# Attention and feed-forward on one core: v of the last batch planned later, mask products a bank wide, the last output in column halves, priorities anew

## The chip, the core and the metric

The kernel runs on one core of one Trainium2 chip. A core has five engines with a queue of instructions each: TensorE (matmuls; PE in the profile, with its weight loads as PEld), VectorE (DVE), ScalarE (ACT), GpSimd (POOL) and SyncE (SP), and 16 DMA engines. POOL and SP issue the DMAs here. Matmuls write to PSUM, which has 8 banks of 2 KB a partition (512 fp32 columns); SBUF holds everything else. The metric is the time of one execution on the device in microseconds, lower is better.

## The reference

Two things follow one another: an attention with two fixed masks, and a feed-forward layer over its output.

```python
B, H, S, D = 8, 8, 576, 64
scores = q @ k.T / sqrt(D)                    # for each batch and head
rel = pos[:, None] - pos[None, :]
mask_local   = (rel >= 0) & (rel < 32)                        # heads 0 to 3
mask_strided = (rel >= 0) & (pos[None, :] % 32 == pos[:, None] % 32)  # heads 4 to 7
attn = softmax(where(mask, scores, -1e9))
x = (attn @ v), reshaped to 4608 tokens x 512
h = x @ w_in                                  # 512 -> 2048
g = s * max(h, 0)**2 + b
out = g @ w_out                               # 2048 -> 512, fp32
```

Inputs and output are fp32 in DRAM; the kernel computes in fp16 with sums in fp32.

## The kernel before

**How the work is cut.** A batch has two pairs of local heads (m = 0, 1) and two of strided heads (m = 2, 3). A local pair is 6 tiles of 96 queries; a tile sees its own 96 keys and the 32 before them, so 128 key rows. A strided pair is 8 tiles of 72: positions that are equal modulo 32 meet only each other, and four such classes share a tile of 72. Two heads lie side by side, so one scores product has 2 x 96 or 2 x 72 columns, and a PSUM bank takes two local tiles (384 columns) or three strided ones (432). `pair_steps` (L474) lists the TensorE steps of a pair: transposes of q and k (L494, L502, with the results copied or spread over tiles by `copy_on`, L404), scores (L623), the exponential on ScalarE (L641), the products with v (L684; a column of ones in v gives the sum of each row), reciprocal (L701) and normalising (L707 on ScalarE, six instructions of 96x64 a group, allowed for batch 0 only, or L711 on VectorE, one instruction), and the transposes of x (L731). In later batches the transposes of q, k and x are DMA transposes on SP's queue; q then goes through a spreading copy.

**The mask.** For batches 1 to 7 VectorE multiplies the exponentials by a mask of 0 and 1 (L649). For batch 0 (`b < PE_MASK`) TensorE writes the mask ahead of each scores product: identity times a row of 0 and -30000 (L620), with the scores product then added in the same columns of PSUM.

**v.** `fetch_v` (L1339) issues the loads of v of a batch on POOL's queue, four DMAs for local heads (L382) and, from batch 4 on, four for strided heads (L387). In the local form each tile of v has the last 32 rows of the tile before it as its first rows; `rows_before` (L435) copies them, in two instructions a batch, on ScalarE or VectorE (kind "in"). They are due when the plan expects the loads to have landed: `landing(4600)`.

**The feed-forward.** `ff1` (L973) multiplies 128 of 2048 rows by a block of 512 tokens (matmul L983, relu L1009 or L1011, square L1017 or L1019). The last two blocks (T = 7, 8) go through `ff1_seven` (L1087, matmul L1208), which forms the block product with seven half-size products in place of eight. `ff2` (L1229, matmul L1238) and, for later blocks, `ff2_seven` (L853, matmul L951; seven products P1 to P7) do the second product. In `ff2_seven` `ev` (L870) evicts sums that are used twice, `add_db` (L893) adds the bias part, and `store` (L878) evicts a quarter of the output block and issues its DMA on SP (L886). For the last block the bank W is in halves of 128 tokens, and its last product, P3, stores a half after each t.

**Order.** All of it is laid out at build time by a list scheduler, `Plan` (L19). It keeps a clock that TensorE's steps advance, times at which ScalarE, VectorE, GpSimd and the queues are planned to be free, and for each piece of work what it needs and what it costs. `flush` (L45) issues, out of the work that is ready, the piece with the smallest sum of its ready time and an offset in ns for its kind, `ORDER` (L124); work of batch 0 or of first tiles has no offset. An engine may be booked up to `SLACK` ahead. What TensorE does next is chosen in the main loop (L1508): a step of attention if it is ready and either attention is behind its due time (`due`, L1515) or nothing else is ready, else a step of `ff1` or `ff2`; in the head, small products of no use (L1502) keep TensorE running. PSUM banks are given out by `group_of` (L453): one bank for transposes (t), two for scores (s), one for sums over v (a), two each for `ff1` and `ff2`; for batch 0, scores may also use the `f1` banks. No search runs at build (`ORDERS = 0`), so the numbers in `ORDER` settle the order of all instructions.

Of the kernel before, what the change touches and what calls it, by code (L numbers as in the profile page):

```python
# [13 lines left out]
FP32 = mybir.dt.float32  # L14
# [4 lines left out]
class Plan:  # L19
# [98 lines left out]
class Step:  # L118
    def __init__(self, fn, ns, needs=(), group=None, keys=(), posts=(), after=None):
# [4 lines left out]
ORDER = {"g": 1500.0, "S": 2500.0, "in": 2500.0, "w_mix": 0.0, "wc": 1000.0, "ev": 1000.0,  # L124
# [3 lines left out]
         "u": 0.0, "SLACK": 600.0, "ahead": 0.05}  # L128
KINDS = ("g", "S", "in", "w_mix", "wc", "Va", "Ua", "Ub", "Vb", "C22", "xc", "q", "k", "r", "x", "e",
         "p", "u", "ev", "fv", "fu", "fe", "c11", "c22", "c21", "c12")  # L130


def varied(order, rnd):

    order = dict(order)
    for kind in rnd.sample(KINDS, rnd.choice((1, 2, 4))):
        order[kind] = rnd.choice((-1500.0, -800.0, -400.0, 0.0, 500.0, 1000.0, 1500.0, 2500.0))
    if rnd.random() < 0.2:
        order["SLACK"] = rnd.choice((400.0, 600.0, 800.0, 1000.0))
    if rnd.random() < 0.2:  # L140
        order["ahead"] = rnd.choice((0.0, 0.05, 0.1, 0.2))
    return order
# [46 lines left out]
def lay_out(ctx, tc, nc, q, k, v, moe_w_in, moe_w_out, moe_s, moe_b, out, order, q_shape, out_shape,  # L189
# [284 lines left out]
    def pair_steps(b, m):  # L474
# [135 lines left out]
        def score(i, group):  # L610
# [3 lines left out]
            def f():  # L614
                if i % per_s == 0:
                    st["s", g] = bank(group)
                c = i % per_s * 2 * nq
                if b < PE_MASK:

                    nc.tensor.matmul(  # L620
                        out=st["s", g][0:nk, c:c + 2 * nq], lhsT=ident[0:nk, 0:nk],
                        rhs=neg_loc if loc else neg_str, start=True, stop=False)
                nc.tensor.matmul(  # L623
                    out=st["s", g][0:nk, c:c + 2 * nq], lhsT=(st["k"][:, i * nq:i * nq + nk] if loc else st["k"][:, i, 0:SQ]),
                    rhs=st["q"][:, i].rearrange("d e c -> d (e c)"), start=b >= PE_MASK, stop=True)
# [227 lines left out]
    def ff2_seven(T):  # L853
# [24 lines left out]
        def store(i, k, of, plus, ts=slice(0, 2)):  # L878
            def g(eng):
                o = op.tile([128, 2, 256], FP32, tag="o", name="o")  # L880
                src = gts[of, T][:, ts] if (of, T) in gts else gts[of, T, ts.start]
                nc.vector.scalar_tensor_tensor(
                    out=o[:, ts], in0=src, scalar=s_sb[:, 0:1],
                    in1=plus()[:, ts], op0=ALU.mult, op1=ALU.add)
# [3 lines left out]
                        "(t p) m -> p t m", p=128)[:, ts], in_=o[:, ts])  # L888
# [707 lines left out]
```

## Time and profile before

| | |
|---|---|
| median of 3 runs | 298.67 us (298.17 to 298.99) |
| profiled execution | 298.86 us |
| its span, first to last instruction | 297.1 us |
| granted TensorE clock | 0.999 of full speed |
| TensorE busy from 9 to 20.4 us | 10.39 us |
| TensorE busy from 20.4 to 174 us | 153.60 of 153.6 us |
| TensorE busy from 174 to 204 us | 29.23 of 30 us |
| TensorE busy from 242 to 293.6 us | 51.58 of 51.6 us |
| last matmul ends | 293.58 us |
| last DMA, 128 KB of output, issued and landed | 294.13 and 296.18 us |

The first rows are the whole run; the stretches show where TensorE has gaps. The ends of matmuls are modelled, so "busy" is not "at its peak": how densely matmuls stand is read from their starts. A few lines of the costliest groups, with busy time and mean ns of one, then the idle time of the engine ahead of them and what ended it:

```profile
L983 PE MATMUL ps_f<-xT,w_in_sb 128*128 128x512 f16 (+4 forms) x568 | 115.5, 331 | 0.3 <-ACT u L1009 0.3
L1009 ACT ACTIVATE u<-ps_f 128x512 f16<-128x512 f32 x104 | 61.0, 594 | 32.5 <-PE ps_f L983 31.8
L951 PE MATMUL ps_f<-w_out_sb,gT 128*128 128x256 f16 x376 | 55.6, 273 | 0.0
L641 ACT ACTIVATE p_loc<-ps_s 128x384 f16<-128x384 f32 x46 | 21.4, 494 | 4.8 <-PE ps_s L623 4.3
```

TensorE's first product hardly ever waits (0.3 us in the whole run), and ScalarE's relu spends its idle time waiting for TensorE.

### The profile page before, as it was taken

The numbers are of one execution on the slowest core, as the hardware profiler recorded it, in microseconds if no ns is written. First come the engines' busy times: TensorE is split into PE (matmuls) and PEld (weight loads), VectorE is DVE, ScalarE is ACT, GpSimd is POOL, SyncE is SP. The second block draws the span as 40 slices with busy tenths as digits, with TensorE's granted clock in tenths as the row PEclk, the third lists the DMA queues.
The fourth block names the chain that finished last, engine by engine and source line by source line (L and its number), as shares of the span: only waits on it lengthen the run. The fifth ranks groups of instructions, "written<-read, shape, count | busy, mean of one in ns | idle before, by whom it ended". The sixth has DMA issues, their size and how long they took to land.

```text
span 297.1 us, 7092 instructions
## 1 busy us (share of the span) xinstructions
PE 290.5 (98%) x2802; PEld 220.0 (74%) x2802; DVE 235.3 (79%) x501; ACT 194.3 (65%) x336; POOL 93.7 (32%) x140
## 2 busy tenths in 40 slices
PE   8999999999999999999999999999999999999995
PEld 3775656666556568889767776768888989999984
DVE  5857888798966988787877896759898588888963
ACT  3577957898838798647774878469877545675400
POOL 8873624601980296009710394100000000000000
PEclk9999999999999999999999999999999999999999
DMA  8999999997999499989999999999230300110214
GB/s 136 189 206 203 218 180 184 223 171 119 109 195 149 67 132 138 170 173 122 148 136 144 182 170 105 143 140 207 44 97 0 108 29 9 71 38 3 95 48 142
DMA packets 106152, 38.19 MB, mean 129 GB/s; under 512 B 85414, under 2 KB 103974, under 8 KB 106118
## 3 DMA queue, kind: packets, MB, share of 16 engines
q0 software_dynamic: 60848, 18.23, 62.7%
q1 hardware_dynamic: 45270, 19.51, 36.0%
q8 instruction: 22, 0.36, 0.5%
q14 instruction: 12, 0.10, 0.1%
HBM read 36.99 MB, written 10.62 MB: 160 GB/s over the span
## 4 chain that ended last, share of the span: by engine, by line
PE 88%; DMA 6%; ACT 2%; DVE 2%; POOL 1%; issue 1%; ACTq 0%
PE ps_f L983 28%; PE ps_f L951 22%; PE ps_f L1238 8%; DMA v_loc<-in_v_dram 6%; PE ps_s L623 5%; PE ps_f L1208 3%; PE ps_a L684 3%; PE ps_s L1502 2%; PE ps_a L1208 2%; PE ps_s L951 2%; PE ps_t L1208 2%; PE ps_s L1208 2%; PE ps_t L951 1%; PE ps_s L1238 1%; PE ps_t L684 1%; PE ps_t L502 1%
## 5 line engine op out<-in xcount | busy, mean ns | idle before, releaser
L983 PE MATMUL ps_f<-xT,w_in_sb 128*128 128x512 f16 (+4 forms) x568 | 115.5, 331 | 0.3 <-ACT u L1009 0.3
L1009 ACT ACTIVATE u<-ps_f 128x512 f16<-128x512 f32 x104 | 61.0, 594 | 32.5 <-PE ps_f L983 31.8
L983 PEld LDWEIGHTS <-w_in_sb 128*128 128x128 f16 x576 | 57.4, 114 | 23.2 <-issue 0.5
L951 PEld LDWEIGHTS <-gT 128*128 128x128 f16 x608 | 58.4, 98 | 9.2
L951 PE MATMUL ps_f<-w_out_sb,gT 128*128 128x256 f16 x376 | 55.6, 273 | 0.0
L1017 ACT ACTIVATE gT<-u 128x1024 f16<-128x1024 f16 x29 | 30.7, 1057 | 0.8
L1238 PE MATMUL ps_f<-w_out_sb,gT 128*128 128x512 f16 x112 | 30.4, 379 | 0.0
L951 PE MATMUL ps_f<-w_mix,gT 128*128 128x256 f16 x176 | 25.1, 273 | 0.0
L641 ACT ACTIVATE p_str<-ps_s 72x432 f16<-72x432 f32 (+1 forms) x46 | 20.7, 482 | 6.4 <-PE ps_s L623 5.8
L711 DVE TENSOR_TENSOR x_nat<-ps_a,rec 96x384 f16<-96x384 f32 (+2 forms) x46 | 24.1, 523 | 0.6
L641 ACT ACTIVATE p_loc<-ps_s 128x384 f16<-128x384 f32 x46 | 21.4, 494 | 4.8 <-PE ps_s L623 4.3
L1019 DVE TENSOR_TENSOR gT<-u 128x1024 f16<-128x1024 f16 x27 | 18.5, 686 | 5.9 <-ACT u L1009 5.4
L819 DVE TENSOR_TENSOR gT<-gT 128x1024 f16<-128x1024 f16 x34 | 22.4, 678 | 0.6 <-ACT gT L1017 0.4
L382 POOL DMA_DIRECT2D v_loc<-in_v_dram x24 | 17.7, 757 | 8.6 <-DMA w_out_sb<-in_moe_w_out_dram 5.7
L951 PEld LDWEIGHTS <-S 128*128 128x128 f16 x176 | 17.1, 98 | 2.9
L1238 PEld LDWEIGHTS <-gT 128*128 128x128 f16 x128 | 11.4, 98 | 7.8
L387 POOL DMA_DIRECT2D v_str<-in_v_dram x16 | 13.0, 816 | 12.3 <-PE ps_f L983 3.6
L684 PEld LDWEIGHTS <-p_str 72*128 72x128 f16 x256 | 12.8, 98 | 5.1 <-ACT p_str L641 0.4
L1323 POOL COPY gate<-kT 1x1 f16<-1x1 f16 x6 | 1.5, 256 | 45.0 <-DMA kT<-ks 45.0
L951 PE MATMUL ps_f<-w_mix,S 128*128 128x256 f16 x112 | 15.5, 273 | 0.0
L701 DVE RECIPROCAL rec<-ps_a 96x6 f32<-96x6 f32 (+2 forms) x47 | 8.6, 182 | 8.6 <-PE ps_a L684 8.4
L1149 ACT ACTIVATE gT<-u 128x1024 f16<-128x1024 f16 x12 | 12.7, 1058 | 1.7 <-DVE u L1128 1.4
(237 smaller groups left out, 529.7 us busy)
## 6 DMA issues: line engine op xcount, KB each, us to landing
out_dram<-o SPq DMA_DIRECT2D x34, 256.0 KB, 2.9
w_in_sb<-in_moe_w_in_dram POOLq DMA_DIRECT2D x4, 512.0 KB, 9.7
w_out_sb<-in_moe_w_out_dram POOLq DMA_DIRECT2D x4, 512.0 KB, 9.9
qs<-in_q_dram POOLq DMA_DIRECT2D x6, 288.0 KB, 8.4
ks<-in_k_dram POOLq DMA_DIRECT2D x6, 288.0 KB, 9.7
v_loc<-in_v_dram POOLq DMA_DIRECT2D x24, 72.0 KB, 9.6
ql<-in_q_dram POOLq DMA_DIRECT2D x4, 288.0 KB, 9.0
kl<-in_k_dram POOLq DMA_DIRECT2D x16, 72.0 KB, 3.6
```

The source lines that it names most:

```text
L382: nc.gpsimd.dma_start(out=vl[LPAD:128, h, :, 0:D], in_=v_band(b, h))
L641: nc.scalar.activation(out=st["pw", g][0:nk, 0:2 * n * nq], in_=st["s", g][0:nk, 0:2 * n * nq], func=AF.Exp, scale=scale)
L684: nc.tensor.matmul(out=st["pa", g][:, n % 6, :], lhsT=st["pw", gp_][0:nk, i * nq:i * nq + WIDE], rhs=vt[0:nk, 2 * mm + e, j, :])
L711: nc.vector.tensor_tensor(out=x_at(0, cnt), in0=st["pa", g][0:nq, 0:cnt, 0:D], in1=st["rec", g][0:nq, 0:cnt].to_broadcast([nq, cnt, D]), o ...
L819: {"V": nc.vector, "P": nc.gpsimd}[eng].tensor_tensor(out=at(out), in0=at(x), in1=at(y), op=op)
L951: nc.tensor.matmul(out=gts[name, T, t][:, 0] if halves else gts[name, T][:, t], lhsT=lhs(k, t), rhs=rhs(k), start=fresh and k == 0 and (ha ...
L983: nc.tensor.matmul(out=gts["h", T, ft][:, lo:hi], lhsT=w_in_sb[ft // 4][:, ct].rearrange("p (x l) -> p l x", l=4)[:, ft % 4], rhs=xT[ct][: ...
L1009: nc.scalar.activation(out=u, in_=gts["h", T, ft], func=AF.Relu)
L1017: nc.scalar.activation(out=g, in_=u, func=AF.Square)
L1019: nc.vector.tensor_tensor(out=g, in0=u, in1=u, op=ALU.mult)
L1208: nc.tensor.matmul(out=st[bk][:, 256 * t:256 * t + 256], lhsT=lhs(t, c), rhs=rhs(c), start=fresh and t == c == 0, stop=t == c == 1, skip_g ...
L1238: nc.tensor.matmul(out=gts[id_], lhsT=gts[T][:, ft, ts * 128:(ts + 1) * 128], rhs=w_out_sb[:, ft, cols], start=(ft == 0), stop=(ft == NFT ...
```

## The change

Five things change.

1. *v of the last batch.* In `fetch_v` the planned arrival of v of batch B - 1 is 5,000 ns later, for local and strided heads. The DMAs are the same.
2. *Mask products of batch 0.* A new step, `forbid`, writes the mask over a whole bank (384 or 432 columns, fewer in the last one of a strided pair) with one matmul, ahead of the bank's two or three scores products. It only needs the mask itself, which the plan expects at 5,000 ns; the step that took the bank was a scores product before, which also needs q and k. The scores products of batch 0 no longer have a mask product of their own.
3. *The last output.* The last product P3 of the last block runs as before for t = 0 (256 columns); for t = 1 it runs in two column halves of 128, each with its own eviction and its own DMA. `store` takes a slice of columns, and the halves of a quarter share one buffer `o` in SBUF; before, each half had a buffer of its own from the pool of three.
4. *Priorities.* `flush` takes its offset from `late`: work of batch 0 can now have an offset of its own ("q01" is q of batch 0, pair 1; "invl00" the rows of v), else none as before; other work has one for its kind as before, but of new values. `SLACK` goes from 600 to 400.
5. *Due times.* `ahead` goes from 0.05 to 0.2, with a further offset for each sixth of the way (`ahead0` to `ahead5`), and `lead`, the distance at which `ff2` goes before `ff1`, from 1 to 1.1.

Loops in `flush` that only look differently, and the code for a search that isn't run, are left out here.

```diff
+    def late(self, k):
+
+        if not isinstance(k, tuple):
+            return 0.0
+        at = k[1] if len(k) > 1 and isinstance(k[1], tuple) else k[2:4] if k[0] == "in" else ()
+        if len(at) == 2 and at[0] == 0:
+            own = k[0] + (k[1] if k[0] == "in" else "") + "0" + str(at[1])
+            if own in self.LATER:
+                return self.LATER[own]
+        return 0.0 if k[2:3] == (0,) else self.LATER.get(k[0], 0.0)
+
     def flush(self):
         while True:
             best = None
             for p in self.pend:
-                r = self.ready_at(p[0])
-                if r is None or r > self.t:
-                    continue
-                if p[1].keys() <= {"A", "V"} and min(
-                        self.free[e] for e in p[1]) > self.t + self.SLACK:
-                    continue
-                k = p[3][0]
-                w = r + self.LATER.get(k[0] if isinstance(k, tuple) and k[2:3] != (0,) else None, 0.0)
-                if best is None or w < best[0]:
-                    best = (w, r, p)
+                r = 0.0
+                for k in p[0]:
+                    v = self.done.get(k)
+                    if v is None or v > self.t:
+                        break
+                    r = max(r, v)
+                else:
+                    if p[1].keys() <= {"A", "V"} and min(
+                            self.free[e] for e in p[1]) > self.t + self.SLACK:
+                        continue
+                    w = r + self.late(p[3][0])
+                    if best is None or w < best[0]:
+                        best = (w, r, p)
             if best is None:
...
-ORDER = {"g": 1500.0, "S": 2500.0, "in": 2500.0, "w_mix": 0.0, "wc": 1000.0, "ev": 1000.0,
-         "c21": 1500.0, "c11": 500.0, "c12": 500.0, "C22": -1500.0, "fv": 0.0, "Vb": -400.0,
-         "x": -1500.0, "Ub": 1000.0, "xc": -1500.0, "fe": -400.0, "k": 1500.0, "fu": -1500.0,
-         "Va": 500.0, "p": 0.0, "c22": 500.0, "Ua": 2500.0, "e": -1500.0, "q": 0.0, "r": 0.0,
-         "u": 0.0, "SLACK": 600.0, "ahead": 0.05}
+ORDER = {"g": 1000.0, "S": 2500.0, "in": 1000.0, "w_mix": -400.0, "wc": 1500.0, "ev": -800.0,
+         "c21": 0.0, "c11": -800.0, "c12": -400.0, "C22": 500.0, "fv": 500.0, "Vb": -800.0,
+         "x": -800.0, "Ub": -1500.0, "xc": -800.0, "fe": 1500.0, "k": 1500.0, "fu": -800.0,
+         "Va": 500.0, "p": -1500.0, "c22": 0.0, "Ua": 0.0, "e": -1500.0, "q": 2500.0,
+         "r": -800.0, "u": 0.0, "q01": 2500.0, "p00": 500.0, "x00": -1500.0, "invl01": 0.0,
+         "invs00": 1000.0, "k01": 2500.0, "r02": 1500.0, "lead": 1.1, "ahead4": 0.1,
+         "r00": 1500.0, "x01": -800.0, "invl00": 2500.0, "invs01": 1500.0, "q02": 1500.0,
+         "r03": -400.0, "q03": 500.0, "ahead3": 0.05, "p02": -800.0, "k02": 500.0,
+         "r01": -1500.0, "p03": 1500.0, "q00": 500.0, "p01": -1500.0, "k00": 1500.0,
+         "x02": 500.0, "ahead2": -0.15, "ahead5": -0.15, "k03": 1000.0, "ahead0": -0.05,
+         "ahead1": -0.15, "SLACK": 400.0, "ahead": 0.2}
...
             def f():
-                if i % per_s == 0:
+                if i % per_s == 0 and b >= PE_MASK:
                     st["s", g] = bank(group)
                 c = i % per_s * 2 * nq
-                if b < PE_MASK:
-
-                    nc.tensor.matmul(
-                        out=st["s", g][0:nk, c:c + 2 * nq], lhsT=ident[0:nk, 0:nk],
-                        rhs=neg_loc if loc else neg_str, start=True, stop=False)
                 nc.tensor.matmul(
                     out=st["s", g][0:nk, c:c + 2 * nq], lhsT=(st["k"][:, i * nq:i * nq + nk] if loc else st["k"][:, i, 0:SQ]),
-                    rhs=st["q"][:, i].rearrange("d e c -> d (e c)"), start=b >= PE_MASK, stop=True)
-
-            s = Step(f, (2 if b < PE_MASK else 1) * (2 * nq / 2.4 + 8), needs=[("q", id_), ("k", id_)],
-                     group=group if i % per_s == 0 else None)
+                    rhs=st["q"][:, i].rearrange("d e c -> d (e c)"), start=b >= PE_MASK, stop=True,
+                    skip_group_check=b < PE_MASK)
+
+            s = Step(f, 2 * nq / 2.4 + 8, needs=[("q", id_), ("k", id_)],
+                     group=group if i % per_s == 0 and b >= PE_MASK else None)
...
+        def forbid(i, group):
+
+            n = min(per_s, nt - i)
+
+            def f():
+                st["s", i // per_s] = bank(group)
+                nc.tensor.matmul(
+                    out=bank(group)[0:nk, 0:2 * n * nq], lhsT=ident[0:nk, 0:nk],
+                    rhs=(neg_loc if loc else neg_str)[:, None, :].to_broadcast([nk, n, 2 * nq]),
+                    start=True, stop=False, skip_group_check=True)
+            return Step(f, 2 * n * nq / 2.4 + 3, needs=[("negs",)], group=group)
+
         gr = None
         for i in range(nt):
             if i % per_s == 0:
                 gr = group_of("s", b, m)
+                if b < PE_MASK:
+                    steps.append(forbid(i, gr))
             steps.append(score(i, gr))
...
-        def store(i, k, of, plus, ts=slice(0, 2)):
+        def store(i, k, of, plus, ts=slice(0, 2), ms=slice(0, 256)):
             def g(eng):
-                o = op.tile([128, 2, 256], FP32, tag="o", name="o")
+                if (of, T) in gts or (i, k, "o") not in gts:
+                    gts[i, k, "o"] = op.tile([128, 2, 256], FP32, tag="o", name="o")
+                o = gts[i, k, "o"]
                 src = gts[of, T][:, ts] if (of, T) in gts else gts[of, T, ts.start]
                 nc.vector.scalar_tensor_tensor(
-                    out=o[:, ts], in0=src, scalar=s_sb[:, 0:1],
-                    in1=plus()[:, ts], op0=ALU.mult, op1=ALU.add)
+                    out=o[:, ts, ms], in0=src[:, :, ms], scalar=s_sb[:, 0:1],
+                    in1=plus()[:, ts, ms], op0=ALU.mult, op1=ALU.add)
                 r0 = T * PS + 256 * i
                 nc.sync.dma_start(
                     out=out[r0:r0 + 256, 256 * k:256 * k + 256].rearrange(
-                        "(t p) m -> p t m", p=128)[:, ts], in_=o[:, ts])
+                        "(t p) m -> p t m", p=128)[:, ts, ms], in_=o[:, ts, ms])
             return g
...
-            for t in range(2):
-                for k in range(H):
+            ends = [(t, k, slice(0, 256)) for t in range(2) for k in range(H)]
+            if last and key == "P3":
+                ends = ends[0:H] + [(1, k, slice(128 * c, 128 * c + 128)) for c in range(2)
+                                    for k in range(H)]
+            for t, k, ms in ends:
+                if True:
                     halves = last and name == "W"
 
-                    def f(k=k, t=t, group=group, name=name, fresh=fresh, lhs=lhs, rhs=rhs, key=key,
+                    def f(k=k, t=t, ms=ms, group=group, name=name, fresh=fresh, lhs=lhs, rhs=rhs, key=key,
                           halves=halves):
                         if halves and fresh and k == 0:
                             gts[name, T, t] = bank(Ws[t])[:, None, 0:256]
                         elif fresh and t == k == 0:
                             gts[name, T] = bank(group).rearrange("p (t m) -> p t m", t=2)
-                        nc.tensor.matmul(out=gts[name, T, t][:, 0] if halves else gts[name, T][:, t],
-                                         lhsT=lhs(k, t), rhs=rhs(k),
+                        dst = gts[name, T, t][:, 0] if halves else gts[name, T][:, t]
+                        nc.tensor.matmul(out=dst[:, ms], lhsT=lhs(k, t), rhs=rhs(k)[:, ms],
                                          start=fresh and k == 0 and (halves or t == 0),
                                          stop=t == 1 and k == H - 1, skip_group_check=True)
-                    s = Step(f, 110, needs=needs(k) + ([(x[0], T, t) if halves and x == d("C22")
+                    s = Step(f, 110 if ms.stop - ms.start == 256 else 57, needs=needs(k) + ([(x[0], T, t) if halves and x == d("C22")
                                                         else x for x in more]),
                              group=(Ws[t] if halves else group) if fresh and k == 0 and
                              (halves or t == 0) else None)
                     if k == H - 1 and key == "P3" and last:
-                        s.keys = [("P3", T, t)]
-                        s.posts = [([("P3", T, t)], {"V": 420.0},
-                                    store(0, 1, "W", val("Ub"), slice(t, t + 1)),
-                                    [Ws[t]])]
+                        s.keys = [("P3", T, t, ms.stop)]
+                        s.posts = [([("P3", T, t, ms.stop)],
+                                    {"V": 480.0 if ms.stop - ms.start == 256 else 280.0},
+                                    store(0, 1, "W", val("Ub"), slice(t, t + 1), ms),
+                                    [Ws[t]] if ms.stop == 256 else [("P3", T)])]
                     elif t == 1 and k == H - 1:
                         s.keys = [d(key)]
                         s.posts = posts
-                    if t == 1 and k == H - 1 and key == "P3":
+                    if t == 1 and k == H - 1 and key == "P3" and ms.stop == 256:
                         s.keys = s.keys + [("F2", T)]
...
     def fetch_v(b):
         load_vl(b)
-        plan.done["raw", "vl", b] = landing(4600)
+        late = 5000.0 if b == B - 1 else 0.0
+        plan.done["raw", "vl", b] = landing(4600) + late
         for mm in range(2):
             rows_before(b, mm, ("raw", "vl", b))
         if b < LONG_V:
             early_v(b)
         else:
             load_vs(b)
-            arrive(both("vs", b), landing(5000))
+            arrive(both("vs", b), landing(5000) + late)
...
+    plan.done["negs",] = 5000.0
...
     def due():
 
         pos = f1_pos[i1] + (f2[i2 - 1].pos if i2 else 0.0) + plan.ahead
+        pos += order_.get(f"ahead{int(pos / 3)}", 0.0)
         return (pos if pos <= 1 else 1 + (pos - 1) / 2) * batch_ns
...
+    order_, lead = order, order.get("lead", 1.0)
...
-        if len(order) == 2 and i1 % 4 == 0 and f1_pos[i1] > (f2[i2 - 1].pos if i2 else 0.0) + 1:
+        if len(order) == 2 and i1 % 4 == 0 and f1_pos[i1] > (f2[i2 - 1].pos if i2 else 0.0) + lead:
```

More of the change, by code (lines that the diff above doesn't have):

```diff
@@ L121, in __init__ @@
         self.keys, self.posts, self.after = keys, posts, after
-ORDER = {"g": 1500.0, "S": 2500.0, "in": 2500.0, "w_mix": 0.0, "wc": 1000.0, "ev": 1000.0,
[3 rows of a table removed]
-         "u": 0.0, "SLACK": 600.0, "ahead": 0.05}
+ORDER = {"g": 1000.0, "S": 2500.0, "in": 1000.0, "w_mix": -400.0, "wc": 1500.0, "ev": -800.0,
[9 rows of a table added]
+         "ahead1": -0.15, "SLACK": 400.0, "ahead": 0.2}
 KINDS = ("g", "S", "in", "w_mix", "wc", "Va", "Ua", "Ub", "Vb", "C22", "xc", "q", "k", "r", "x", "e",
          "p", "u", "ev", "fv", "fu", "fe", "c11", "c22", "c21", "c12")
+HEAD = tuple(f"{x}0{m}" for x in ("q", "k", "r", "x", "p") for m in range(4)) + tuple(
+    f"in{x}0{m}" for x in ("vl", "vs") for m in range(2))
 def varied(order, rnd):
     order = dict(order)
-    for kind in rnd.sample(KINDS, rnd.choice((1, 2, 4))):
+    for kind in rnd.sample(KINDS if rnd.random() < 0.6 else HEAD, rnd.choice((1, 2, 4))):
         order[kind] = rnd.choice((-1500.0, -800.0, -400.0, 0.0, 500.0, 1000.0, 1500.0, 2500.0))
@@ L141, in varied @@
         order["ahead"] = rnd.choice((0.0, 0.05, 0.1, 0.2))
+    if rnd.random() < 0.2:
+        order[f"ahead{rnd.choice(range(6))}"] = rnd.choice((-0.15, -0.1, -0.05, 0.0, 0.05, 0.1))
+    if rnd.random() < 0.1:
+        order["lead"] = rnd.choice((0.9, 1.0, 1.1, 1.25))
     return order
```

## The prediction

> **What bounds the kernel now.** I read in this order: the page's busy line, the busy time by stretches, TensorE's waits, the chain of waits around the one DMA in it, and the timelines at the head, that place and the end.
>
> ```profile
> PE 290.5 (98%) x2802; PEld 220.0 (74%) x2802; DVE 235.3 (79%) x501; ACT 194.3 (65%) x336; POOL 93.7 (32%) x140
> ```
>
> TensorE is the bound. Start to start, its matmuls stand at 216 ns (512 columns), 109 (256), 82 (192), 56 (128) for all but a few from 20.4 to 293.6 us. Whatever delays one of them there delays the end by as much; what runs on another engine only counts if TensorE waits for it. So the question is where TensorE loses time. Its waits, the whole run (us in total, times, longest):
>
> ```profile
> PE ps_f L623 <- DVE kTs L404: 0.5, 1, 0.5
> PE ps_s L623 <- ACT p_loc L641: 0.4, 1, 0.4
> PE ps_f L983 <- ACT u L1009: 0.3, 1, 0.3
> PE ps_f L684 <- ACT p_str L641: 0.3, 1, 0.3
> PE ps_a L1208 <- ACT E L404: 0.2, 1, 0.2
> ```
>
> Ends of matmuls are modelled, so I price a stall from start to start, less the usual step: 0.69 us at 13.7 (kTs), 0.43 at 18.1 (p_str), 0.15 at 174.95, 0.51 at 196.03 (u), 0.58 at 199.92 (p_loc), 0.40 at 239.2 (E). After 20.4 us that is 1.64 us in all. The pair at 196 and 200 has one cause; the chain of waits, then the timeline:
>
> ```profile
> 178.55 16.76 DMA v_loc<-in_v_dram
> ...
> 195.39 0.12 ACT v_loc L404
> 195.51 0.51 issue
> 196.02 0.59 ACT u L1009
> ```
> ```profile
> 195.39 0.73 ACT L404 COPY v_loc<-v_loc 32x640 f16<-32x640 f16 x1 [2.47 <-DMA v_loc<-in_v_dram]
> ...
> 196.66 1.02 PE L983 MATMUL ps_f<-xT,w_in_sb 128*128 128x512 f16 x4 [0.35 <-ACT u L1009]
> ...
> 200.61 0.32 PE L623 MATMUL ps_s<-qD_loc,kT_alt 128*128 128x192 f16 x2 [0.42 <-ACT p_loc L641]
> ```
>
> ScalarE stood 2.47 us before a copy of rows of v of batch 7 whose transfer landed at 195.3; the relu behind it (L1009) came late, TensorE had no free bank; the late ScalarE work then held up the exponentials (L641).
>
> At the head a transfer sets a second limit, which matters for the change:
>
> ```profile
> 26.81 0.57 PEld L494 LDWEIGHTS <-ql 96*64 96x64 f16 x24 [0.41 <-DMA ql<-in_q_dram]
> ```
>
> q of batch 1 landed at 26.4 (issued at 17.0, 9.4 to landing), 0.4 us before TensorE was there. Nothing before it can pay more than that, unless the order is different there; it isn't: both lists have the same 32 matmuls of the first product ahead of these transposes.
>
> **What the Trainium skill says.** "TensorE: Matmul & The Clock Gate", section "Wait — 56ns, not 53.3ns?", gives columns over 2.4 GHz plus about 2.5 ns from start to start, warm; the trace has 216 and 56 ns. So a product over a whole bank saves only the 2.5 ns of each instruction that goes. The same page's table of specifications has ScalarE and VectorE as strict first-in first-out: the 2.47 us above is that. "PSUM — Partial Sum Buffer", section "The four PSUM rules", says that the first matmul of a group clears written-bits over the whole bank and later ones add where bits are set: one mask product of up to 432 columns, then scores added, is in order; no run shows it yet. "DMA: Bandwidth & Descriptors", section "Anatomy of one DMA", has about 2 us fixed for a transfer; the last store (128 KB) took 2.05 us from issue at 294.13 to landing at 296.18, 64 KB more or less cannot matter much.
>
> **The change, part by part.**
>
> *v of batch 7 planned 5 us later.* The rows copies move behind: against the batch-7 scores, the ScalarE copy goes from ahead of the spreading of q to behind it; counted in TensorE's work back from the end, it stands at 199.0 instead of 194.4, and the second (now VectorE) at 199.8. The transfers do not move: the same POOL list, 0.72 us an issue, started by the same transposes of batch 6 on SP (161.5 to 164 us), so the last lands at about 195.3 again, 2.7 us ahead even if everything runs 1.7 us early. That cover gone, ScalarE would wait again, one for one after some 1.9 us. Gain: 0.51 + 0.58 = 1.09. Both places are late by ScalarE's wait alone, so I take the whole; from the other side 0.5, if the second bank wait has a share of its own.
>
> *What it puts next on SP.* For batch 7 the transposes now go qTl, qTl, kT, kT, qT2, qT2, xT2 (batch 6), a store, kT2, kT2, xT3; before, both kT2 went ahead of xT2. kT2 landed at 202.9 and 203.5 (issued 195.4 and 197.1) and its scores ran at 204.2. In the new order the store that stood before qT2 is out of the way (about 1 us) and xT2 (1.2 to 2.3 us) is in: kT2 issues between 194.3 and 197 and lands between 202 and 204.5; its scores would be at 203.2. Cost 0 to 1.3; I take 0.
>
> *Mask products.* 28 become 12, columns stay 4,608: 16 times 2.5 ns, 0.04 us. Worth more is that each now stands before the scores, where TensorE waits for q and k, and takes the place of fillers: the first exponential can start 0.17 us earlier (two scores, not two masks and two scores, after 8.86).
>
> *Head, order anew.* The row to see:
>
> ```profile
> 11.67 1.32 ACT L707 ACTIVATE x_nat<-ps_f,rec 96x64 f16<-96x64 f32 x6 [1.02 <-DVE rec L701]
> 12.86 0.88 ACT L641 ACTIVATE p_loc<-ps_s 128x384 f16<-128x384 f32 x2
> ```
>
> These six move to VectorE as one of 0.55, so the second pair's exponentials start after their scores, near 11.4 and not 12.86. VectorE gains that and one kTs (0.46) and loses one spread of q (0.91). Following both queues: k of pair 1 at 10.3 to 11.06 (before 10.78 to 11.54), the two x_nat to 12.4, q spread to 13.3, xT to 13.75, kTs to 14.2 and 14.65: the stall at 13.7 to 14.4 remains at about 0.4. Exponentials end near 17.7 instead of 18.8. The last x_nat on ScalarE ends at 20.1, and the third column block of the first product starts near 21.0 instead of 21.75: 0.75 earlier. From there to the transposes of q of batch 1 are 24 matmuls of 216 ns: 26.2, and the landing at 26.4 holds them to about 26.45 instead of 26.81. Gain 0.35; from below -0.5 (VectorE 0.8 later than I make it), from above 0.4. w_in (17.1, 19.6, 22.8, 25.2) and w_out (34.9 to 42.8) land ahead of their new use; v of batch 1 lands at 45.4 with its products near 46.5: no cost.
>
> *The end.* The last 8 matmuls of 109 ns become 16 of 56: 0.02 more. The eviction goes from 0.48 to about 0.35 (0.75 at 512 columns and 0.48 at 256 leave 0.21 fixed). SP needs some 0.4 an issue, so the second half is issued at about 294.05 instead of 294.13; with half the bytes behind it I take 0.25, between 0.05 and 0.45. One buffer for both halves adds waits: the store of product P4 now waits for both 128 KB transfers, landed 291.2 and 291.6; it started at 291.87. Nothing.
>
> *Priorities elsewhere.* 0.15 at 174.95 and 0.40 at 239.2 are of the plan's kind, small mistakes of a list that is otherwise tight; new lists make their own. I let these two stand and add one of 0.3. From below -0.55, from above 1.5. The q spread that leaves POOL at 79 us (two copies, 3.4 us there) is 1.3 on ScalarE, which has gaps there.
>
> **Sum.** 1.09 + 0.35 + 0.25 + 0.04 - 0.3 = 1.4 us. The profiled execution took 298.86 (span 297.1, 1.76 around it); it becomes 297.4. The median shown is 298.67, 0.19 lower; I predict 297.3.
>
> **Rivals.**
> *A, a new wait takes the gain.* kT2 lands at 204.5 (xT2's place in the queue) and a second small stall comes in the reordered middle: 1.4 - 1.3 = 0.1, 298.6. For: 202.9 against a use at 204.2 is tight, and TensorE arrives earlier. Against: 1 us of the SP queue is freed.
> *B, slower: SP decides.* The same queue, worse: transposes issued between 180 and 191 took 7 to 11 us to land, because v's transfers fill the DMA engines till 202. If kT2 keeps the 9 us of qT2 and issues at 198, it lands at 207, 3.8 us after its turn: -1.4 + 3.8 = +2.4, 301. It decides from a landing at 206 on (203.2 plus the 2.7 us that make 0.9 slower). Against: landings were catching up (4.4 for xT2).
> *C, more.* The plan also loses the stalls at 175 and 239, the end pays 0.45, no new stall: 0.4 + 1.09 + 0.55 + 0.45 = 2.5, 296.2.
>
> **Numbers.** Forecast 0.58, A 0.2, B 0.12, C 0.1. About 0.3% (0.9 us) is what a measurement can tell: faster 0.68 (the forecast and C), same 0.2, slower 0.12. The range runs from C's 296.2 to 299.3, which leaves out B and a little; the forecast alone is 296.7 to 297.8.
>
> **What would show it.** Right: the wait of ScalarE for v_loc near 195 is gone, TensorE shows no wait between 194 and 202; the first transposes of q of batch 1 start at 26.45 with a wait for that DMA; the last store is two of 64 KB, ending 0.2 to 0.3 us sooner after TensorE's last matmul. Wrong: these transposes after 26.9 (head), TensorE waiting for kT2 near 203, or several new waits over 0.3 us between 30 and 175.

## The result, and the profile after

The changed kernel took 300.35 us (median of 6 runs, 299.87 to 301.49), the kernel before 298.42 (6 runs, 297.88 to 298.99): ratio 1.0067, interval 1.0045 to 1.0090. It is slower by 1.9 us; 297.3 was predicted, with a range to 299.3. The profiled execution of the changed kernel took 299.88 (span 298.1), 0.47 under its median, so its trace shows less than the whole loss. Runs more than 1.5% above the fastest of their kernel are left out of the ratios below.

The busy line, then TensorE's waits (engine, line, what for: us in total, times, longest):

```profile
PE 289.3 (97%) x2794; PEld 218.8 (73%) x2794; DVE 238.6 (80%) x506; ACT 192.2 (64%) x331; POOL 90.3 (30%) x138
```
```profile
PE ps_t L522 <- DMA ql<-in_q_dram: 1.9, 2, 1.2
PE ps_f L996 <- DVE o L922: 1.2, 1, 1.2
...
PE ps_s L646 <- DMA kT<-ks: 0.2, 1, 0.2
```

All the entries that I had priced are gone: no wait for a relu (u) or for p_loc, none for E at 239. Two large ones are new. Priced from start to start, as before: 1.35 us at 26.2 before the transposes of q of batch 1, 0.34 at 203.8 before the strided scores of batch 7 (kT), and 1.41 at 292.8, in the middle of the very last product. The stalls at 175 and 239 (0.15 and 0.40), which I had let stand, are gone too.

The first of the new ones, in TensorE's weight loads:

```profile
27.78 0.57 PEld L522 LDWEIGHTS <-ql 96*64 96x64 f16 x24 [1.67 <-DMA ql<-in_q_dram]
```

TensorE came to these at 26.44 (the matmul ahead starts at 26.22 and takes 0.216), 0.28 us sooner than in the profile of before; but q landed at 27.74 in this execution instead of 26.4. The last one, in the timeline of the end (start, duration, engine, what, and the wait ahead of it):

```profile
289.18 6.33 SPq L926 DMA_DIRECT2D out_dram<-o  x7
...
292.23 0.83 PE L996 MATMUL ps_f<-w_out_sb,S 128*128 128x128 f16 x12
292.85 0.75 DVE L922 SCALAR_TENSOR_TENSOR o<-ps_f,sb_all,Ua 128x512 f32<-128x512 f32 x1 [2.29 <-DMA out_dram<-o]
293.52 0.47 DVE L922 SCALAR_TENSOR_TENSOR o<-ps_a,sb_all,Ub 128x256 f32<-128x256 f32 x1
293.91 0.34 DVE L922 SCALAR_TENSOR_TENSOR o<-ps_f,sb_all,Ub 128x128 f32<-128x128 f32 x1
294.31 0.38 PE L996 MATMUL ps_f<-w_out_sb,S 128*128 128x128 f16 x4 [1.25 <-DVE o L922]
```

Read it from the last line up. The last four matmuls, of the second column half, wait for VectorE's eviction of the first column half. Both halves lie in one bank of PSUM. That eviction stands in VectorE's queue behind the evictions of P3's t = 0 and of P4 (the line with Ua), and P4's waited 2.29 us for a store to land. In the kernel before it waited for its own operand:

```profile
291.87 0.75 DVE L882 SCALAR_TENSOR_TENSOR o<-ps_f,sb_all,Ua 128x512 f32<-128x512 f32 x1 [1.00 <-PE ps_f L951]
```

P4's eviction needs a buffer o, and it gets the one that both halves of the quarter C22 now share. That it gets this one follows from the code, and "The change" does not say it: `store` makes a new buffer for a half only when there is none under `(i, k, "o")`, and this key has no block number in it. The block before has left its own there. So the halves of C22 and of P3 of the last block go on in the buffers that the block before made for these two quarters, the quarter of P2 takes the third, and P4 has to take over that of C22, once both of its stores have landed. If the key had the block in it, P4's turn would come to the buffer of the block before's P3, whose store was issued at 281.86; no kernel of this kind was run.

The chain of waits says the same in order of time:

```profile
289.65 3.08 DMA out_dram<-o
292.73 0.03 issue
...
292.85 0.06 DVE o L922
```

The store issued at 289.65 took 3.08 us, where the same one took 1.79 before (issued 289.94, landed 291.73). The trace has 16 landings for each of these stores, and the core has 16 DMA engines; I take each to be the part of one engine. In this trace 15 parts of the two stores had landed by 290.91 and 291.39, and one part of each came at 292.42 and 292.73. In the kernel before the last part came within 0.05 us of the one ahead of it. So one DMA engine seems to have been busy with something else. The DMA queues of a stretch show what (queue, kind: packets, MB, share). First the kernel before, 288.4 to 290 us, then the changed kernel, 290 to 291.6:

```profile
q8 instruction: 1, 0.02, 4.8%
```
```profile
q1 hardware_dynamic: 274, 0.25, 45.5%
q8 instruction: 1, 0.02, 5.1%
```

One packet of 16,384 bytes on a queue of its own: a block of instructions. Before, it is alone in its stretch (288.55 to 289.77), ahead of the stores' data; in the changed kernel it runs from 290.14 to 291.46 among them. "Runtime: NRT & Kernel Launch" in the Trainium skill, section "Instruction fetch mechanics", says that an engine's instructions come in blocks of 16 KiB, 256 instructions, and calls the cost mostly hidden. The trace agrees on the block and its spacing: a matmul comes with a weight load, so 256 instructions are 128 matmuls; the kernel before has 22 such packets for its 2,802 matmuls, and at its end 118 to 130 matmuls from one packet to the next. That the changed list has 16 mask products less is then enough to move the last block later against the end of the work, by 16 matmuls of 109 ns, 1.7 us (an estimate; against the issue of the first of the two stores it moved by 1.9 us). The experiments below show a cost that the page doesn't speak of: not a wait of TensorE for its instructions, but a late part of stores in flight.

### The profile page after: what moved, and what is told of

It is laid out like the page before. It is cut to its first block, busy times and chain, and to the rows that moved or that the text cites. A ratio compares the mean times of both kernels' runs of the same rounds, so it can differ in the third digit from the quotient of the medians.

```text
span 298.1 us, 7078 instructions
## 1 busy us (share of the span) xinstructions
PE 289.3 (97%) x2794; PEld 218.8 (73%) x2794; DVE 238.6 (80%) x506; ACT 192.2 (64%) x331; POOL 90.3 (30%) x138
## 4 chain that ended last, share of the span: by engine, by line
PE 84%; DMA 10%; POOL 3%; DVE 1%; issue 1%; SPq 0%; DVEq 0%; POOLq 0%
PE ps_f L1028 30%; PE ps_f L996 22%; PE ps_f L1283 8%; PE ps_s L646 4%; DMA ql<-in_q_dram 3%; PE ps_f L1253 3%; DMA kT<-ks 3%; DMA vs<-in_v_dram 3%; PE ps_a L722 2%; PE ps_a L1253 2%; PE ps_s L996 2%; PE ps_s L1253 2%; PE ps_t L1253 2%; PE ps_s L1283 1%; PE ps_t L722 1%; DMA out_dram<-o 1%
## 5 line engine op out<-in xcount | busy, mean ns | idle before, releaser
L996 PE MATMUL ps_f<-w_out_sb,gT 128*128 128x256 f16 x376 | 54.9, 273 | 0.0
L1283 PE MATMUL ps_f<-w_out_sb,gT 128*128 128x512 f16 x112 | 29.8, 379 | 0.0
L1062 ACT ACTIVATE gT<-u 128x1024 f16<-128x1024 f16 x27 | 28.5, 1057 | 0.7
L749 DVE TENSOR_TENSOR x_nat<-ps_a,rec 96x384 f16<-96x384 f32 (+2 forms) x45 | 23.4, 520 | 0.5
L1064 DVE TENSOR_TENSOR gT<-u 128x1024 f16<-128x1024 f16 x29 | 19.8, 683 | 3.5 <-ACT u L1054 3.4
L1194 ACT ACTIVATE gT<-u 128x1024 f16<-128x1024 f16 x11 | 11.6, 1059 | 2.4 <-DVE u L1173 2.3
```

The source lines that it names most:

```text
L749: nc.vector.tensor_tensor(out=x_at(0, cnt), in0=st["pa", g][0:nq, 0:cnt, 0:D], in1=st["rec", g][0:nq, 0:cnt].to_broadcast([nq, cnt, D]), o ...
L996: nc.tensor.matmul(out=dst[:, ms], lhsT=lhs(k, t), rhs=rhs(k)[:, ms], start=fresh and k == 0 and (halves or t == 0), stop=t == 1 and k == ...
L1062: nc.scalar.activation(out=g, in_=u, func=AF.Square)
L1064: nc.vector.tensor_tensor(out=g, in0=u, in1=u, op=ALU.mult)
L1283: nc.tensor.matmul(out=gts[id_], lhsT=gts[T][:, ft, ts * 128:(ts + 1) * 128], rhs=w_out_sb[:, ft, cols], start=(ft == 0), stop=(ft == NFT ...
```

## The experiments

**Undo or add one part: e1 to e4.** e1 is the changed kernel with the last output as in the kernel before, column halves and shared buffers both undone:

```diff
-            if last and key == "P3":
+            if False and last and key == "P3":
...
-                if (of, T) in gts or (i, k, "o") not in gts:
+                if True:
```

> The changed kernel with its last product P3 and its stores as before: 256 columns for each t, a buffer of its own for each half; all else is the same list. Theory E (the end): the second column half waits for the eviction of the first half, which lies in the same bank, and that one stands behind the store of P4, which waits for a buffer; so the 1.35 us gap in TensorE at 292.8 goes: 0.6 to 1.5 us less than the changed kernel, 299.0 to 299.7, and the last matmul again follows without a wait. Rival T (transfers only): the gap was one late transfer of that execution; the time stays within 0.3 us of the changed kernel's 300.35. For the head, which is the same as in the changed kernel: if its wait for q of batch 1 belongs to the order, TensorE again waits over 0.8 us there; if it was one execution's slow transfers, the q of batch 1 lands nearer 26.4 and the wait is under 0.5.

298.61 us, ratio to the kernel before 1.0003 (0.9982 to 1.0023). The whole loss was in the last output; theory E is right in place and larger than I gave it. q of batch 1 landed at 26.94 and TensorE stood 0.54 there, not 1.35: most of that wait belongs to the execution's transfers. The late parts of the stores are still there (291.65 and 291.96 against 289.97 and 290.47 for the other 15), and P4's eviction still waited 2.15 us, but no matmul stood behind it:

```profile
291.77 0.75 DVE L922 SCALAR_TENSOR_TENSOR o<-ps_f,sb_all,Ua 128x512 f32<-128x512 f32 x1 [2.15 <-DMA out_dram<-o]
```

e2 is the changed kernel without the later plan for v, e3 the kernel before with only that (`late = 5000.0 if b == B - 1 else 0.0` in `fetch_v`, set to 0 or added).

> The changed kernel without the 5,000 ns for v of batch 7; the list is the same up to 170 us. Theory V (v planned later is worth the two stalls at 196 and 200): 1.0 to 1.2 us slower than the changed kernel, 301.4, with ScalarE or VectorE waiting for v_loc near 195 and TensorE standing after it. Rival O (the new priorities move these copies anyway, or what stands behind them is not urgent): within 0.4 us of 300.35, and the wait for kT at 203.8 (0.34 us) is smaller or gone.

> The kernel before with only the 5,000 ns for v of batch 7. Theory V: the two stalls at 196 and 200 go, 1.09 us, and kT costs up to 0.4: 0.7 to 1.1 us faster than before, ratio 0.9965 to 0.998. Rival K (SP's queue takes the gain): kT of batch 7 lands after its turn by 1 us or more, ratio 0.999 to 1.003. TensorE waits for q of batch 1 in the head as in the kernel before, about 0.4 us, if transfers are steady from run to run.

e2: 300.99, ratio 1.0078 (1.0058 to 1.0099), some 0.6 us more than the changed kernel; the two intervals overlap, and in the profiles the end alone differs by 0.76 us (a gap of 2.17 against 1.41, with a longer fetch), so this doesn't show what the later plan is worth there. e3: 300.0, ratio 1.0039 (1.0020 to 1.0058): slower, where theory V and rival K both had less. TensorE's waits in e3:

```profile
PE ps_s L1208 <- DVE qD_loc L1083: 0.8, 1, 0.8
...
PE ps_s L623 <- ACT p_loc L641: 0.4, 1, 0.4
```

From start to start these are 0.94 at 230.8 and 0.55 at 203.2. Neither is a wait for v. At 230.8 TensorE waits for sums that VectorE forms for the seven-product blocks (L1083), because other work was put ahead of them; at 203 ScalarE's exponentials stand behind a copy that spreads q, and this copy waited 0.85 us for its transpose. e2 has the same 0.94 at 228.5, 0.47 at 202.7, and no stall between 194 and 202. So the 5,000 ns act through where the plan puts everything after them: alone they cost about 1.2 us (0.39% of 298.5).

e4 is the kernel before with the column halves and the shared buffers alone.

> The kernel before with only the last output in column halves of one buffer; all else is the same list. Theory E: a gap in TensorE before the last four products of 0.4 us at least and 1.4 where the store of P4 waits for a buffer too: 0.3 to 1.3 us slower, ratio 1.001 to 1.0045. Rival as predicted at first (shorter eviction and half the bytes, no wait): 0.25 us faster, ratio 0.9992.

299.04, ratio 1.0018 (1.0000 to 1.0035): 0.5 us slower, at the edge of what can be told. The end of e4:

```profile
291.82 0.83 PE L958 MATMUL ps_f<-w_out_sb,S 128*128 128x128 f16 x12
292.69 0.35 DVE L884 SCALAR_TENSOR_TENSOR o<-ps_f,sb_all,Ub 128x128 f32<-128x128 f32 x1 [0.19 <-PE ps_f L958]
293.10 0.38 PE L958 MATMUL ps_f<-w_out_sb,S 128*128 128x128 f16 x4 [0.44 <-DVE o L884]
```

The eviction of the first half starts when 12 of the 16 short matmuls are done, and the last four wait for it: a gap of 0.61 us from start to start. The fetch ran from 288.02 to 289.33, ahead of the data, and both stores landed whole (290.52, 291.10), so this gap is the bank's wait alone. Part of it comes back: from the start of the last matmul to the last landing it is 2.33 us, and 2.86 in the kernel before.

**The fetch and the buffer: e5 to e8.** e5 cuts 8 of the products of no use in the head into three, so that 16 matmuls are added and nothing else changes:

```diff
+        cuts = (1, 1, 2) if n == 4 and cut_up[0] else (n,)
+        cut_up[0] -= len(cuts) > 1
...
+            for c in cuts:
                 nc.tensor.matmul(
-                    out=out, lhsT=ones16, rhs=ones16[:, None, :].to_broadcast([128, n, 128]),
+                    out=out[:, 128 * at:128 * (at + c)], lhsT=ones16,
+                    rhs=ones16[:, None, :].to_broadcast([128, c, 128]), start=True, stop=True)
```

e6 is the changed kernel with `bufs=4` for the pool `op`, every instruction in the same order.

> The changed kernel with 8 of its products of no use in the first 6 us cut into three each (512 columns into 128, 128 and 256): 16 more matmuls, the same columns, all other instructions the same. Theory F (a fetch of instructions): TensorE's instructions come in 16 KB, one such transfer for every 128 matmuls; in the changed kernel one runs at 290.1 to 291.5 on one DMA engine and holds up that engine's part of the two stores issued at 289.2 and 289.6 by 1.6 us; in the kernel before it runs at 288.6 to 289.8, ahead of their data. 16 matmuls more bring it 1.7 us earlier: both stores land whole by 291.5, the eviction of P4 starts at about 291.6, TensorE's gap before the last four products falls from 1.4 to 0.4 to 0.6, and the time by 0.8 to 1.2 us, to 299.2 to 299.6. Rival B (the late part belongs to the stores themselves or to one slow engine): the part stays 1.6 us late, the gap at 1.4 and the time within 0.3 us of 300.35.

> The changed kernel with four buffers o for the output in place of three, every instruction in the same order. Theory F with the buffer as the link: the part of the stores is still late (292.4), but the eviction of P4 no longer waits for it; TensorE's gap falls to 0.4 to 0.6 and the time by 0.8 to 1.2, to 299.2 to 299.6. Rival P (the wait is only for the bank of PSUM and the eviction in it, the buffer doesn't matter): gap 1.2 to 1.5 as before, 300.35.

e5: 298.26, ratio 0.9998 (0.9974 to 1.0023). e6: 298.25, ratio 0.9994 (0.9973 to 1.0016). Either one takes off 2.1 us, about twice what theory F had (0.8 to 1.2). In e5 the last block of instructions came from 287.82 to 288.75 and both stores landed whole. The end of e5:

```profile
290.84 0.75 DVE L922 SCALAR_TENSOR_TENSOR o<-ps_f,sb_all,Ua 128x512 f32<-128x512 f32 x1 [1.00 <-PE ps_f L996]
...
292.79 0.38 PE L996 MATMUL ps_f<-w_out_sb,S 128*128 128x128 f16 x4 [0.44 <-DVE o L922]
```

and of e6:

```profile
290.32 0.75 DVE L922 SCALAR_TENSOR_TENSOR o<-ps_f,sb_all,Ua 128x512 f32<-128x512 f32 x1 [0.99 <-PE ps_f L996]
...
292.27 0.38 PE L996 MATMUL ps_f<-w_out_sb,S 128*128 128x128 f16 x4 [0.44 <-DVE o L922]
```

What ends the wait of P4's eviction is in both the matmul that makes its operand, and no longer a store; the 0.61 us of the bank stay (start to start). In e6 the parts are as late as ever (291.51 and 291.84). The collision delays one part; the shortage of buffers carries the delay to VectorE; the bank's wait carries it to TensorE. Over the profiles (us; "15" and "16" are the landings of the last but one and of the last part):

| kernel | fetch | two stores issued | first: 15 / 16 | second: 15 / 16 | P4's eviction starts |
|---|---|---|---|---|---|
| before | 288.55-289.77 | 289.49, 289.94 | 291.19 / 291.23 | 291.72 / 291.73 | 291.87 |
| after | 290.14-291.46 | 289.18, 289.65 | 290.91 / 292.42 | 291.39 / 292.73 | 292.85 |
| e2 | 290.22-291.85 | 289.06, 289.53 | 290.79 / 293.16 | 291.28 / 293.36 | 293.48 |
| e5 | 287.82-288.75 | 288.47, 288.94 | 290.16 / 290.21 | 290.70 / 290.71 | 290.84 |
| e6 | 289.01-290.38 | 287.95, 288.42 | 289.68 / 291.51 | 290.17 / 291.84 | 290.32 |

All 14 profiles agree with theory F. In seven (the changed kernel, e1, e2, e6, e10, e11, e12) the fetch began 0.9 to 1.2 us after the first of the two stores was issued, and one part of both came late, 1.0 to 1.3 us after the end of the fetch for the first. In the other seven it began 0.6 to 1.0 us ahead of that issue, and no part was late.

> The kernel of e1 (last output as in the kernel before) with the same 16 more matmuls in the first 6 us. Theory F: in e1 the fetch still made the eviction of P4 late (2.15 us of waiting for a store, 291.77) and its last matmul was followed by 4.07 us of evictions and stores, against 3.5 in the kernel before; with the fetch out of the way it is 3.5 again: 0.4 to 0.6 us less than e1's 298.61, about 298.1, ratio to the kernel before 0.9982 to 0.9992. Rival B: as e1, 1.0003.

e7 (e1 with e5's cut): 297.88, ratio 0.9980 (0.9960 to 0.9999). As theory F has it, though the intervals of e1 and e7 overlap.

e8 puts the first column half ahead of t = 0 and the second behind it, with four buffers and e5's cut:

```diff
-                ends = ends[0:H] + [(1, k, slice(128 * c, 128 * c + 128)) for c in range(2)
-                                    for k in range(H)]
+                cols = [[(1, k, slice(128 * c, 128 * c + 128)) for k in range(H)] for c in range(2)]
+                ends = cols[0] + ends[0:H] + cols[1]
```

> The changed kernel with the first column half of t = 1 ahead of t = 0 and the second behind it, four buffers o, and the 16 more matmuls. Theory E: the 8 products of t = 0 (0.87 us) now lie over the eviction of the first half, so there is no gap in TensorE at the end, and the last eviction is of 128 columns (0.35 instead of 0.48) with half the bytes to store: 0.1 to 0.3 us less than e7, 297.8 to 298.1, ratio 0.997 to 0.9988. Rival: SP's three issues, 0.4 to 0.5 us each, set the end and take it back: as e7 or 0.2 slower.

297.92, ratio 0.9981 (0.9963 to 0.9999). The end of e8:

```profile
292.17 0.61 PE L996 MATMUL ps_f<-w_out_sb,S 128*128 128x128 f16 x8
292.37 0.48 DVE L922 SCALAR_TENSOR_TENSOR o<-ps_a,sb_all,Ub 128x256 f32<-128x256 f32 x1 [0.31 <-PE ps_a L996]
292.81 0.35 DVE L922 SCALAR_TENSOR_TENSOR o<-ps_f,sb_all,Ub 128x128 f32<-128x128 f32 x1
```

All eight matmuls of the second half follow without a gap. From the start of the last matmul to the last landing it is 2.40 us, and 2.53 in e7: 0.13 us gained, and the medians don't show it. Whether SP's issues take anything back can't be told from these.

**What the prediction stood on: e9 to e12.** e9 is the kernel before, unchanged.

> The kernel before once more, unchanged, for a second profile of it. Theory L (the two stalls at 196 and 200, 1.09 us, were a late landing of v in the one profiled execution): v of batch 7 lands near 192 to 194, as in e4, and there is no stall there or less than 0.3 us; the time is 297.9 to 298.5. Rival (they belong to the list): both stalls again, 0.5 us each, v at 195.

297.83 in its one run. v of batch 7 landed at 192.3 and ScalarE copied it without a wait:

```profile
192.29 0.60 ACT L1009 ACTIVATE u<-ps_f 128x512 f16<-128x512 f32 x1 [1.03 <-PE ps_f L983]
192.91 0.73 ACT L404 COPY v_loc<-v_loc 32x640 f16<-32x640 f16 x1
```

There is no stall at 196 or 200, and e4, whose list is the same up to the last product, has none either (v at 192.1). In these three profiles of one list v of batch 7 landed at 192.1, 192.3 and 195.3; over all 14, with their different lists, it landed between 192.1 and 196.6, q of batch 1 between 26.2 and 27.7.

e10 is the kernel before with only the wide mask products; e11 is the changed kernel with the priorities and due times of the kernel before, the last output whole and four buffers; e12 is e11 with the new priorities.

> The kernel before with only the mask products of batch 0 a bank wide: 17 matmuls fewer in the list. Theory F: the last fetch of TensorE's instructions moves 1.8 us later against the end, to about 290.2, and falls on the stores issued at 289.5 and 289.9; one part of each lands 1 to 2 us late, the eviction of P4 waits for the first of them, and the end of the run takes 0.3 to 0.7 us more after the last matmul; with 0.2 us gained in the head the ratio is 1.000 to 1.002. Rival (mask products as predicted, a gain of 0.04 to 0.2 us and nothing else): no late part, ratio 0.999 to 1.000.

> The changed kernel with the priorities and due times of the kernel before, the last output whole and four buffers o, so that the end costs nothing: v late and wide masks alone. Theory N (the new priorities are worth what they save at 228 to 240 and in the head): 0.5 to 1.5 us slower than e12, ratio to before 1.000 to 1.004, with stalls like those of e3 near 203 and 230. Rival (priorities are worth nothing): as e12, within 0.3 us.

> The changed kernel with the last output whole as in the kernel before and four buffers o; the fetch stays where the changed kernel has it. Theory F with the buffer as the link: the parts of the stores are late, but nothing waits for them, so it is as fast as e7, where the fetch was moved: 297.7 to 298.2, ratio 0.997 to 0.9985. Rival (the fetch costs by itself, by holding up the last stores too): as e1, 298.6.

e10: 306.26, far off both expectations, and not one clear time: two of its six runs took 301.9 us, four took 306.2 to 307.5 at a granted clock of 0.990 to 0.994. The ratio, 1.0181 (1.0114 to 1.0249), is of two runs of each kind. I have no profile of a long one, so these stay unexplained; the profiled run took 301.9, 3.5 us more than the kernel before. TensorE's waits in it:

```profile
PE ps_f L993 <- ACT u L1019: 1.0, 1, 1.0
PE ps_s L1218 <- DVE qD_loc L1093: 0.8, 1, 0.8
PE ps_f L1248 <- ACT gT L1027: 0.7, 1, 0.7
```

Start to start they are 1.16 at 195.2, 0.94 at 231.6 and 0.89 at 82.5, near 3.0 us. The first is the wait for v of batch 7 that the prediction priced, come again; v landed at 195.2:

```profile
195.24 0.72 ACT L404 COPY v_loc<-v_loc 32x640 f16<-32x640 f16 x1 [3.12 <-DMA v_loc<-in_v_dram]
```

The fetch (292.26 to 293.63) made one part of each store 1.6 and 1.5 us late, as theory F has it, and P4's eviction started at 294.82, after the first of them. e11: 302.08, ratio 1.0125 (1.0085 to 1.0164), with 0.89 at 83.2, 0.94 at 231.1 and 0.40 at 240.6 in its profile. e12: 297.90, ratio 0.9979 (0.9964 to 0.9994). So the new priorities and due times are worth 4 us to a list with wide masks and v late, where theory N had 0.5 to 1.5; e12's profile has none of these three stalls, 2.2 us together, and the rest isn't explained. e12 is the version to keep, 0.2% faster than the kernel before. The kernel before with four buffers was not run, so what the fourth buffer would give there is open; e7, with three, is as fast as e12. In e12 the fetch still falls on the stores (last parts at 291.98 and 292.34), and P4's eviction, with a buffer to spare, starts at 291.25.

## Why the prediction was wrong

**The end, the step that failed.** The prediction took 0.25 us off and priced the shared buffer at "Nothing", on landings of 291.2 and 291.6 against a start at 291.87. The start had 0.14 us to spare over the later landing, and I had read the landings as if they were fixed. e5 and e6 show that a landing 1.2 to 2.4 us late in one of 16 parts, together with this buffer, costs 2.1 us of the median. Nor does this wait belong to one buffer for both halves as such: by the code, it comes of the key without the block. The gaps in two profiles (1.41 in the changed kernel, 2.17 in e2) are only 0.8 and 1.6 above e5's 0.61; what the other 0.5 to 1.3 us are in a run without a profile stays open. Forecast and result are 3.05 us apart; these 2.1 and the 1.09 for v below make up about that (an estimate).

What I forecast of the tail itself came, and more: from the start of the last matmul to the last landing it is 2.86 us in the kernel before and 2.28 in the changed kernel, or 2.53 in e7 against 2.19 in e5, with halves evicted in 0.35 us against 0.48, as I had it.

**The wait for the bank.** I left it out altogether. e4, e5 and e6 have it where nothing waits for a late store: a gap of 0.61 us in each, more than the 0.3 to 0.5 that the shorter tail gives back. "PSUM — Partial Sum Buffer", section "PSUM bank collisions raise a hardware error", was there to be read: the compiler puts a dependency between instructions of different engines on one bank in the same 32 partitions, and other columns of it collide too. The traces agree: the 13th of the 16 short matmuls waits for an eviction of other columns.

**v of batch 7.** The largest term, 1.09 us, is not there in every run. I took the profile of before as the rule, though the kernel's own median lay under it. With v planned as before and the old priorities, e4 and e9 show no such stall (v at 192.1 and 192.3), and e10 has one of 1.16 us (v at 195.2). The mechanism was right: where v lands late, ScalarE waits and TensorE stands, and in the changed kernel, where v landed only at 196.6, nothing stood between 194 and 202. The size was that of one execution, and e3 shows that the edit alone costs 1.2 elsewhere in the list.

**SP's order (0 to 1.3, taken 0).** In the profiles that share the changed order the stall before kT's scores was 0.2 to 0.8 us in five (the changed kernel, e1, e7, e8, e12) and none in two (e5, e6): inside the bounds, but not 0.

**Head (0.35).** TensorE comes sooner (26.44, where I had 26.2) and the landing of q caps it, as predicted; but the landing moves. Where q is there in time the transposes start at 26.8 before and near 26.4 now (e2, e7); with the 14 landings seen this gains 0.15 us on average, an estimate.

**Mask products (0.04).** The columns cost the same, as predicted (162 to 188 ns for 384 and 432). What they do to the list, and to the place of the fetch, was not in the sum.

**Priorities (-0.3).** The stalls at 175 and 239, 0.55 us together, went, where I let them stand. e12 against the kernel before, -0.46 us in the medians, is of the size of these with the head's little, less kT's wait; no run takes them apart.

Of the rivals, B ended on the right side for a reason that was not there: the two transfers of kT landed at 204.2 and 204.9, not at 207. (Its limit of 206 was mis-summed as well: with 1.4 us of gain it takes 2.3 us of waiting, a landing at 205.5, to be 0.9 slower.) A had that landing nearly right, at 204.5, but a wait of 0.34 us took only a part of what it said. That a transfer would decide was right; the wrong one was named.

## What to carry to other kernels

A buffer that is free 0.14 us ahead of its use is not free: ask which transfer frees it and what else uses the DMA engines then, TensorE's own instructions among it. Before a product is split so that its first part can be evicted early, look at whether both parts lie in one bank. When pieces of work are made to share a buffer, look at how long its key keeps it: here, by the code, it reached back to the block before. A stall in one profile is not the rule until a second profile of the same list shows it too.

## What the runs showed of the hardware that I had not expected

A block of TensorE's instructions, 16,384 bytes, takes 0.9 to 1.6 us on one DMA engine at the end of these runs, and a store that shares this engine has one of its 16 parts 1.2 to 2.4 us late. At the end of the kernel before such a block comes every 118 to 130 matmuls, so taking 16 matmuls away at the head of the kernel moves it against the work at the end, 270 us later; adding 16 matmuls of no use made the changed kernel 2.1 us faster.
